# Float32 on TensorE for the first batch's scores and first weights, and decays summed on 128 partitions

## The chip, the cores and the metric

The kernel runs on one core of a Trainium2 chip. The metric is the device time of one execution in microseconds (us). Five engines run side by side, each with its own queue that is worked off in order: TensorE (PE, matrix products; its weight loads are shown as PEld), VectorE (DVE), ScalarE (ACT), GpSimd (POOL) and SyncE (SP), whose queue issues the DMAs.

## The reference, cut to what matters

```python
scores = q @ k.T / sqrt(64)                       # 4 batches, 8 heads, 576 tokens, 64 columns
cum = cumsum(log(clip(f, 1e-4, 1)), axis=-1)
scores = where(causal, -1e9, scores + cum[..., :, None] - cum[..., None, :])
attn = exp(scores - max); attn /= sum(attn) + 1e-9
x = (attn @ v), heads side by side                # 2304 tokens x 512, float32
h = x @ w_in; g = h * tanh(softplus(h)); y = g @ w_out            # 2048 inner columns
z = (sigmoid(y @ w_gate) * (y @ w_val)) @ w_out2                  # 1536 inner columns
```

## The kernel before, in words

TensorE works in fp16 with float32 sums. To keep precision every operand is a pair, a rounded fp16 part (`hi`) and an fp16 remainder (`lo`), and each product takes three fp16 products; the scores get theirs from two stacked matmuls (`L658` with 128 rows, `L659` with 70 rows; `L717` for the last 64 query rows of a batch). The 70 rows hold, beside the rest of q and k, the decay: three fp16 pieces of `cum` against constants of 8 and -8.

The work is cut by batch (4), by pair of heads (4 a batch, index `p`) and by query chunks of 128 tokens. Batch 0 goes in three parts: chunks 0 and 1 (`part == 0`, called the first part here), chunks 2 and 3, and chunk 4. For each pair the way is: load q and k into `st` (`prep`), split them into pairs (`scaled` on ACT or DVE, `rest` on DVE or POOL), scores on PE (`scores`), masked minimum on DVE (`softmax_part`, `L606`), exponential on ACT (`L674`), split of the weights into the pair `pp` (`split`, `L424` and `L443`), a transposing DMA (`L698`), weights times values on PE (`pv`, `L776`, three fp16 products), and the result into `xt` as a pair (`L797` on ACT, `L800` on DVE). `decay` clips `f`, takes the logarithm, sums along 576 tokens on 32 partitions (`L394`), cuts the sum into three fp16 pieces (`L400`, `L402`), and writes it to DRAM (`cum_d`, `L406`), from where the rows of `sb` and `mb` are read (`L479`, `L481`, later `L486`, `L488`).

Beside it run the two feed-forward stages. `h_stream` (`L865` to `L867`) and `y_stream` (`L898` to `L900`) go through 72 steps of 256 tokens by 256 inner columns; block 0 (tokens 0 to 255) needs the first part of all four pairs of batch 0. The weights come as 64-bit words in 32 tiles of 512 KB (`load_w`, `L564`), are turned into float32 by three instructions on DVE (`L544`, `L548`, `L552`) and split into pairs like the rest. The second feed-forward stage is `gv_stream`.

The order on every engine's queue is made by the class `Order`: each task yields what it is about to do with a planned duration, has a due time, and the planner puts the instructions out one by one; `pick` chooses between ACT, DVE and POOL by planned costs. So an edit of one task moves others too.

Of the kernel before, what the change touches and what calls it, by code (L numbers as in the profile page):

```python
# [7 lines left out]
FP32 = mybir.dt.float32  # L8
FP16 = mybir.dt.float16
# [271 lines left out]
def attention_moe_moe_kernel(ctx, tc, qk, v, f, rows_q, rows_k, w_in, w_out, w_gate, w_val, w_out2, out):  # L281
# [6 lines left out]
    NH = f.shape[0]  # L288
# [89 lines left out]
    cum_d = dram.tile([3, NH, S], FP16, name="cum_d")  # L378

    def decay():  # L380
        ft = words(xt[0], 1280, 2 * S).bitcast(FP32)[0:NH]
        cum = words(xt[0], 1280 + 2 * S, 2 * S).bitcast(FP32)[0:NH]
        c16 = words(win[NG1 - 2], 0, 3 * S).rearrange("p (a s) -> p a s", a=3)[0:NH]
        zt = words(wout[0], 0, 2 * S + 2).bitcast(FP32)[0:NH]
        yield "SP", 0.5, 74000
        nc.sync.dma_start(out=ft, in_=f)
        yield "DVE", t_dve2(S)
        nc.vector.memset(zt, 0.0)
        nc.vector.tensor_scalar(ft, ft, 1.0e-4, 1.0, op0=ALU.max, op1=ALU.min)
        yield "ACT", t_act(S)  # L390
        nc.scalar.activation(out=ft, in_=ft, func=ACTF.Ln)
        nc.scalar.activation(out=zt[:, 0:1], in_=zt[:, 0:1], func=ACTF.Exp, scale=0.0)
        yield "DVE", t_dve(S)
        nc.vector.tensor_tensor_scan(  # L394
            out=cum, data0=ft, data1=zt[:, 1:S + 1], initial=0.0, op0=ALU.add, op1=ALU.add
        )
        for part, (a, b) in enumerate(((0, 256), (256, S))):
            for j in range(3):
                yield "DVE", t_dve2(b - a) + (j < 2) * (t_dve(b - a) + 0.127)
                nc.vector.tensor_copy(c16[:, j, a:b], cum[:, a:b])  # L400
                if j < 2:
                    nc.vector.tensor_tensor(cum[:, a:b], cum[:, a:b], c16[:, j, a:b], op=ALU.subtract)  # L402
            if part == 0:
                done("cum0")
            yield "SP", 0.5, 20000 + part * 20000, ("cum", part)
            nc.sync.dma_start(  # L406
                out=cum_d[:, :, a:b].rearrange("j h s -> h j s"), in_=c16[:, :, a:b]
            )
# [44 lines left out]

    def prep(b, p, part, turn):
        i = b * NPB + p
        c0, n = PART[part]
        if b and part == 0:
            yield from need(("s", b - 1, p))
# [8 lines left out]
        done(("st", i))  # L467
        yield from need(("st", i, part))
        first = b == 0 and part == 0
        keys = [("q", i, part, x) for x in range(4 if first else 7)]  # L470

        def rows():
            yield from need(("cum", part), "cq", "ck")
            o = 2 * i
            if first:

                if p == 0:
                    yield "SP", 0.5, 25000, "rq"
                    nc.sync.dma_start(out=SBt[64:67, :, :, 0:n], in_=cum_d[:, 0:2 * NPB, c0:c0 + n])  # L479
                    yield "SP", 0.5, 25000, "rk"  # L480
                    nc.sync.dma_start(out=MBt[67:70, :, :, 0:n], in_=cum_d[:, 0:2 * NPB, c0:c0 + n])  # L481
                yield from need("rq", "rk")
                done(keys[2], keys[3])
            else:
                yield "SP", 0.5, 10000, keys[2]
                nc.sync.dma_start(out=sb[64:67], in_=cum_d[:, o:o + 2, c0:c0 + n])  # L486
                yield "SP", 0.5, 10000, keys[3]
                nc.sync.dma_start(out=mb[67:70], in_=cum_d[:, o:o + 2, c0:c0 + n])  # L488

        spawn(rows(), od.cur["due"])  # L490
        if first:
# [7 lines left out]
        else:  # L499

            (ci,) = yield from take("low")
            low = at.tile([128, 2, 320], FP16, tag="low", name="low", bufs=BUFS["low"])[:, :, 0:n]
            yield from scaled(ma, st, 1.0, 2 * n)
            for dst, src, key in ((sa[0:64], ma[0:64], 4), (sa[64:128], ma[0:64], 0), (mb[0:64], ma[64:128], 1)):
                yield "SP", 0.68, 256 * n, keys[key]
                nc.sync.dma_start(out=dst, in_=src)
# [914 lines left out]
```

## Time and profile before

| | |
|---|---|
| median of three runs | 953.3 us (952.02 to 954.29) |
| profiled execution | 951.72 us, its span 949.9 us |
| PE busy | 881.4 us, 93% of the span |
| DVE busy | 614.0 us, 65% |
| ACT busy | 568.0 us, 60% |
| POOL busy | 83.5 us |
| HBM read, written | 50.71 MB, 4.83 MB |

The span runs from the first to the last instruction; the profiled execution is 1.8 us longer than it. A busy PE is an engine with a matmul in flight, at either clock.

### The profile page before, as it was taken

To read this page: it belongs to the slowest core of one execution; us is meant where nothing else is said; L and a number is where in the kernel's file an instruction comes from. 1 tells how busy PE (TensorE), PEld (TensorE's weight loads), DVE (VectorE), ACT (ScalarE), POOL (GpSimd) and SP (SyncE) were. 2 spreads that over 40 slices of the span, in tenths; PEclk is the share of its full clock that TensorE was granted. 3 is DMA by queue.
4 is the path that set the end of the run, shared out by engine and by line. 5 is a ranking of instruction groups with operands and counts; after the bars stand their busy time and mean duration, and the time that the engine had idled before them with its cause. 6 is when DMAs were issued, how large, how long until landed. Compare 5 with 4: busy or idle time off the path is not lost.

```text
span 949.9 us, 20753 instructions
## 1 busy us (share of the span) xinstructions
PE 881.4 (93%) x8450; PEld 695.0 (73%) x8450; DVE 614.0 (65%) x1374; ACT 568.0 (60%) x1108; POOL 83.5 (9%) x82
## 2 busy tenths in 40 slices
PE   2376689989999999999999999999999999999998
PEld 1254478868887888877888886777777777777786
DVE  8999969877477756656699999964235332532333
ACT  8678757898688877888454465545324433433343
POOL 0301300120010101100200001200000000000000
PEclk9999899999999999999999999999999999999999
DMA  7687888487557784554444433201000000100000
GB/s 242 163 213 201 213 190 237 95 155 138 119 118 134 129 152 99 126 90 71 104 134 138 152 130 115 67 1 46 1 2 23 23 1 1 46 1 1 12 35 23
DMA packets 153556, 93.58 MB, mean 99 GB/s; under 512 B 109578, under 2 KB 135242, under 8 KB 153456
## 3 DMA queue, kind: packets, MB, share of 16 engines
q1 hardware_dynamic: 153462, 92.27, 40.5%
q8 instruction: 66, 1.08, 0.5%
q14 instruction: 28, 0.23, 0.1%
HBM read 50.71 MB, written 4.83 MB: 58 GB/s over the span
## 4 chain that ended last, share of the span: by engine, by line
PE 64%; DVE 4%; DMA 0%; POOL 0%; ACT 0%; issue 0%; ACTq 0%; POOLq 0%
PE bank L1131 8%; PE bank L1133 8%; PE bank L1132 8%; PE o_acc L1279 4%; PE o_acc L1278 4%; PE o_acc L1277 4%; PE y_ps L898 4%; PE y_ps L900 4%; PE y_ps L899 4%; PE h_ps L865 4%; PE h_ps L867 4%; PE h_ps L866 4%; PE o_ps L776 2%; PE s_ps L658 1%; PE s_ps L659 1%; PE s_ps L717 1%
## 5 line engine op out<-in xcount | busy, mean ns | idle before, releaser
L865 PE MATMUL h_ps<-xt,win 128*128 128x256 f16 x576 | 159.4, 277 | 3.1 <-DVE g L838 2.1
L898 PE MATMUL y_ps<-g,wout 128*128 128x256 f16 x576 | 158.8, 276 | 3.7 <-ACT wout L424 3.6
L899 PE MATMUL y_ps<-g,wout 128*128 128x256 f16 x576 | 158.6, 275 | 3.5 <-DVE wout L443 1.9
L866 PE MATMUL h_ps<-xt,win 128*128 128x256 f16 x576 | 158.9, 276 | 3.1 <-DVE xt L800 2.9
L867 PE MATMUL h_ps<-xt,win 128*128 128x256 f16 x576 | 159.0, 276 | 0.4 <-DVE win L443 0.4
L900 PE MATMUL y_ps<-g,wout 128*128 128x256 f16 x576 | 158.7, 275 | 0.0
L1221 DVE TENSOR_TENSOR v<-bank,e 128x512 f32<-128x512 f32 (+1 forms) x30 | 19.1, 637 | 169.2 <-ACT bank L1138 169.2
L1138 ACT ACTIVATE bank<-bank 128x512 f32<-128x512 f32 (+1 forms) x90 | 48.5, 539 | 93.0 <-PE bank L1133 90.3
L443 DVE SCALAR_TENSOR_TENSOR pp<-sp,sm,pp 128x384 f16<-128x384 f32 (+4 forms) x122 | 78.7, 659 | 17.8 <-ACT pp L424 16.4
L606 DVE CUSTOM_DVE_ANT_0 sp<-s_ps,mask 128x384 f32<-128x384 f32 (+4 forms) x144 | 67.2, 492 | 27.6 <-PE s_ps L659 24.1
L674 ACT ACTIVATE sp<-sp,sm 128x384 f32<-128x384 f32 (+3 forms) x112 | 63.7, 569 | 18.3 <-DVE sm L606 17.7
L424 ACT ACTIVATE pp<-sp,sm 128x384 f16<-128x384 f32 (+4 forms) x115 | 66.2, 599 | 11.1 <-issue 3.8
L865 PEld LDWEIGHTS <-win 128*128 128x128 f16 x576 | 56.9, 99 | 16.6 <-issue 3.4
L898 PEld LDWEIGHTS <-wout 128*128 128x128 f16 x576 | 56.8, 99 | 13.9 <-ACT wout L424 4.2
L867 PEld LDWEIGHTS <-win 128*128 128x128 f16 x576 | 56.9, 99 | 12.0 <-issue 3.9
L899 PEld LDWEIGHTS <-wout 128*128 128x128 f16 x576 | 56.9, 99 | 11.9 <-DVE wout L443 2.3
L866 PEld LDWEIGHTS <-win 128*128 128x128 f16 x576 | 57.0, 99 | 10.7 <-issue 1.7
L776 PE MATMUL o_ps<-pt,vt 128*64 128x128 f16 (+1 forms) x1440 | 48.8, 218 | 16.7 <-DMA pt<-pp 14.9
L776 PEld LDWEIGHTS <-vt 128*64 128x64 f16 x1440 | 39.9, 114 | 31.4 <-issue 21.3
L658 PE MATMUL s_ps<-ma,sa 128*128 128x128 f16 (+3 forms) x128 | 39.1, 322 | 25.0 <-DVE sm L606 12.7
L900 PEld LDWEIGHTS <-wout 128*128 128x128 f16 x576 | 56.9, 99 | 7.1
L838 DVE SCALAR_TENSOR_TENSOR g<-h_ps,g 128x512 f16<-128x512 f32 x72 | 49.0, 684 | 18.8 <-ACT g L834 18.5
(195 smaller groups left out, 2269.0 us busy)
## 6 DMA issues: line engine op xcount, KB each, us to landing
xt<-w_in SPq DMA_DIRECT2D x16, 512.0 KB
xt<-w_out SPq DMA_DIRECT2D x16, 512.0 KB
wraw<-w_gate SPq DMA_DIRECT2D x12, 512.0 KB
wraw<-w_val SPq DMA_DIRECT2D x12, 512.0 KB
wraw<-w_out SPq DMA_DIRECT2D x12, 512.0 KB
st<-qk SPq DMA_DIRECT2D x16, 320.0 KB
out<-ob SPq DMA_DIRECT2D x18, 256.0 KB
st<-qk SPq DMA_DIRECT2D x16, 256.0 KB
```

The costliest lines, as they stand in the source:

```text
L443: nc.vector.scalar_tensor_tensor(dst, a, scale, b, op0=ALU.mult, op1=ALU.subtract)
L606: nc.vector.tensor_tensor_reduce(out=sp, in0=ps_ap, in1=mk, op0=ALU.add, op1=ALU.min, scale=-0.125, scalar=1.0e38, accum_out=mn,)
L776: nc.tensor.matmul(o_ps[64 * hh:64 * hh + 64, col:col + n], lhsT=vv[:, jc, vl, 64 * hh:64 * hh + 64], rhs=ptt[:, k, q0:q0 + n], start=(jc ...
L865: nc.tensor.matmul(dst, lhsT=wh, rhs=xh, start=(k == 0), stop=False)
L866: nc.tensor.matmul(dst, lhsT=wh, rhs=xl, start=False, stop=False)
L867: nc.tensor.matmul(dst, lhsT=wl, rhs=xh, start=False, stop=(k == KD - 1))
L898: nc.tensor.matmul(dst, lhsT=wh, rhs=gh, start=first, stop=False, skip_group_check=True)
L899: nc.tensor.matmul(dst, lhsT=wl, rhs=gh, start=False, stop=False, skip_group_check=True)
L900: nc.tensor.matmul(dst, lhsT=wh, rhs=gl, start=False, stop=last, skip_group_check=True)
L1131: nc.tensor.matmul(dst, lhsT=wh, rhs=xh[:, k], start=first, stop=False, skip_group_check=True)
L1132: nc.tensor.matmul(dst, lhsT=wh, rhs=xl[:, k], start=False, stop=False, skip_group_check=True)
L1133: nc.tensor.matmul(dst, lhsT=wl, rhs=xh[:, k], start=False, stop=last, skip_group_check=True)
```

## The change

Batch 0 keeps q and k in float32. They are loaded straight into `Q32` and `K32`, which are the fp16 buffers of the later batches seen as float32, and one float32 matmul with 66 rows (64 of q and k, two for the decay) stands in place of the two fp16 ones, in all three parts of batch 0. Nothing of q and k is split there, so the staging copies between buffers of that batch fall away too.

In the first part the weights stay in float32 as well. They are not split and not transposed by a DMA: a matmul of the unnormalized weights against a diagonal matrix of the normalizing factors (`diag`, from an identity that is loaded) transposes and scales in one go, ACT or DVE copies the result from PSUM to SBUF, and `pv` multiplies it with float32 values. The values' split is put off until after that.

The decays are summed on 128 partitions, four segments of 144 tokens for each of 32 heads. The Ln instruction also gives each segment's total, one matmul with a matrix of zeros and ones (`carry`, loaded) makes the segments' starting values, and the scan starts from them. The float32 sums of batch 0 go to DRAM at once (`cum_f`) and from there as rows into `Q32` and `K32`, before the cut into fp16 pieces, which only the later batches need. POOL fills two whole rows of `K32` and `Q32` with 8 and -8 (`ones`) before those rows are loaded.

```diff
+def t_pe32(n, cols):
+    return n * (4 * cols / 2400 + 0.003)
...
+    def ones():
+        yield "POOL", 2.5
+        nc.gpsimd.memset(K32[64:KF], 8.0)
+        yield "POOL", 1.5
+        nc.gpsimd.memset(Q32[64:KF], -8.0)
+        done("ones")
...
-        nc.scalar.activation(out=ft, in_=ft, func=ACTF.Ln)
...
+        nc.scalar.activation(out=ft, in_=ft, func=ACTF.Ln, accum_out=tot)
...
+        nc.tensor.matmul(hp, lhsT=cm, rhs=tot, start=True, stop=True)
+        yield "DVE", 0.13
+        nc.vector.tensor_copy(car, hp)
...
+        nc.vector.tensor_tensor_scan(out=cum, data0=ft, data1=zt, initial=car, op0=ALU.add, op1=ALU.add)
+        for seg in range(4):
+            yield "SP", 0.5, 5000, ("cum_f", seg)
+            nc.sync.dma_start(out=cum_f[:, seg * SL:(seg + 1) * SL], in_=cum[seg * NH:seg * NH + 2 * NPB])
...
+    def first_rows():
+        yield from need("ones", ("cum_f", 0), ("cum_f", 1))
+        for key, row, n in (("rq", Q32[64:65], 256), ("rk", K32[65:KF], 256), ("rk2", K32[65:KF], S)):
...
-        if first:
-            yield from scaled(sa[0:64], st[0:64], 1.0, 2 * n, pool=False)
-            yield from scaled(ma[64:128], st[64:128], 1.0, 2 * n, pool=False)
-            yield from scaled(sa[64:128], st[0:64], 1.0, 2 * n, pool=False)
-            yield from scaled(mb[0:64], st[64:128], 1.0, 2 * n, pool=False)
-            done(keys[0], keys[1])
-            yield from rest(ma[0:64], st[64:128], 1.0, ma[64:128], 2 * n)
-            yield from rest(sb[0:64], st[0:64], 1.0, sa[0:64], 2 * n)
...
+    def scores_first(p, turn):
...
+                nc.tensor.matmul(
+                    pst[:, hh * n:hh * n + n], lhsT=Q32[0:KF, hh, qi % NQ, c * 128:c * 128 + 128],
+                    rhs=K32[0:KF, hh, p, 0:n], start=True, stop=True,
+                )
...
+        for k in range(4):
+            yield from scaled(diag[:, k * 128:k * 128 + 128], eye, sm[:, 12 + k:13 + k], 128)
...
+                nc.tensor.matmul(
+                    pst[:, m * 128:m * 128 + 128], lhsT=sps[k][1][:, jc * 128:jc * 128 + 128],
+                    rhs=diag[:, k * 128:k * 128 + 128], start=True, stop=True,
+                )
+            (plan,) = pick([("ACT", t_act(w, 0.05))], [("DVE", t_dve(w))])
...
+                if b == 0:
+                    nc.tensor.matmul(
+                        s, lhsT=Q32[0:KF, hh, qi % NQ, q0:q0 + 128], rhs=K32[0:KF, hh, p, 0:n], start=True, stop=True
+                    )
+                    continue
...
+                if own:
+                    yield "PE", t_pe32(2, 128)
+                    for hh in range(2):
+                        ptt, o, pti = pt_t[i, c, hh]
+                        nc.tensor.matmul(
+                            o_ps[64 * hh:64 * hh + 64, col:col + n],
+                            lhsT=v32[p][:, jc, 64 * hh:64 * hh + 64], rhs=ptt[:, o + jc * 128:o + jc * 128 + n],
+                            start=(jc == 0), stop=(jc == c),
+                        )
+                    continue
```

What the change does to the order is seen at three places. On PE, the program of before began with the scores of the first pair, in fp16 pairs (`sa`, `sb` hold q, `ma`, `mb` hold k):

```order
L658 LDWEIGHTS sa
L658 MATMUL s_ps<-ma,sa 128x128
L659 LDWEIGHTS sb
L659 MATMUL s_ps<-mb,sb 128x128
L658 LDWEIGHTS sa
L658 MATMUL s_ps<-ma,sa 128x128
L659 LDWEIGHTS sb
L659 MATMUL s_ps<-mb,sb 128x128
```

It now begins with the sum of the segments (`L430`), the scores of all four pairs follow, and then come the diagonal products (`L763`), the first score of the next part (`L802`) and the first weights times values (`L927`); the loads of a float32 matmul are not listed:

```order
L430 MATMUL carry_ps<-wout_84 128x1
L716 MATMUL s_ps<-mab,sab 128x128 x2
L716 MATMUL s_ps<-mab,sab 128x256 x2
L716 MATMUL s_ps<-mab,sab 128x128 x2
L716 MATMUL s_ps<-mab,sab 128x256 x2
L716 MATMUL s_ps<-mab,sab 128x128 x2
L716 MATMUL s_ps<-mab,sab 128x256 x2
L716 MATMUL s_ps<-mab,sab 128x128 x2
L716 MATMUL s_ps<-mab,sab 128x256 x2
L763 MATMUL t_ps<-diag,wout_88 128x128 x6
L802 MATMUL s_ps<-mab,sab 128x384
L927 MATMUL o_ps<-pt_195,xt_72 64x128 x2
```

So all sixteen score matmuls of the first part stand ahead of the first diagonal product, and scores of the second part stand between the products of the first.

On SP, the queue of before had, after the load of `f`, the loads of q and k (`st`), the constants, a weight tile, and then the way of the decays through DRAM:

```order
L466 DMA st<-qk 128x2x256
L359 DMA sb<-rows_q 6x2560
L361 DMA mb<-rows_k 6x4608
L466 DMA st<-qk 128x2x256 x3
L564 DMA xt_74<-w_in 128x2x512
L406 DMA cum_d<-win_82 32x3x256
L479 DMA sb<-cum_d 3x8x256
L481 DMA mb<-cum_d 3x8x256
```

Now q and k go to their places by two DMAs each (`mab`, `sab`), and the decays' write and read (`cum_f`) stand among them, with the first weight tile behind:

```order
L519 DMA mab<-qk 64x2x256
L438 DMA cum_f<-xt_71 8x144 x2
L521 DMA sab<-qk 64x2x256
L519 DMA mab<-qk 64x2x256
L521 DMA sab<-qk 64x2x256
L508 DMA sab<-cum_f 1x8x256
L508 DMA mab<-cum_f 1x8x256
L630 DMA xt_74<-w_in 128x2x512
```

The first weight tile moved from ahead of the decays' write to behind the decays' rows.

On DVE, the stretch ahead of the first masked minimum (`L606`) of before was filled with the fp16 pieces of the decays, remainders of q and k (`ma`, `sb`) and the first weight tile (`xt_75`):

```order
L400 CAST win_82<-xt_71 32x320
L443 SCALAR_TENSOR_TENSOR ma<-st,ma 64x2x256
L544 TENSOR_SCALAR xt_75<-xt_74 128x512
L443 SCALAR_TENSOR_TENSOR sb<-st,sa 64x2x256
L443 SCALAR_TENSOR_TENSOR ma<-st,ma 64x2x256
L548 SCALAR_TENSOR_TENSOR xt_75<-xt_74,xt_75 128x512
L443 SCALAR_TENSOR_TENSOR sb<-st,sa 64x2x256
L552 SCALAR_TENSOR_TENSOR xt_75<-xt_74,xt_75 128x512
L443 SCALAR_TENSOR_TENSOR ma<-st,ma 64x2x256
L606 ISA wout_88,sm<-s_ps,mask 128x128
```

Now only the decays' sum and a mask stand ahead of it (`L673` is the same operation):

```order
L422 TENSOR_SCALAR xt_71<-xt_71 128x144
L432 COPY wout_84<-carry_ps 128x1
L435 SCALAR_TENSOR_TENSOR xt_71<-xt_71,wout_84 128x144
L394 MEMSET mask_93 128x144
L395 COPY mask_93<-mask 64x64
L396 COPY mask_93<-mask 64x64
L673 ISA wout_88,sm<-s_ps,mask 128x128
L673 ISA sm 128x1
L673 ISA wout_88,sm<-s_ps,mask 128x128
L673 ISA sm 128x1
L607 TENSOR_SCALAR xt_75<-xt_74 128x512
```

The first weight tile and the fp16 pieces moved behind the first masked minimum, and the remainders are gone.

## Rows read from the trace of the kernel before

**Rows 1.** Busy time by stretch; columns as the header of the view says.

```profile
core 0: us, PE busy (x) PEld busy (x) DVE busy (x) ACT busy (x) POOL busy (x), PEclk, DMA share, GB/s
0.00:51.80 51.80, 17.14 (x122) 10.13 (x123) 46.40 (x123) 39.39 (x96) 9.83 (x12) 1.00 0.75 208
51.80:200.00 148.20, 121.52 (x1266) 96.73 (x1265) 131.13 (x317) 113.88 (x233) 23.66 (x23) 0.96 0.79 187
50.00:57.30 7.30, 6.73 (x42) 4.33 (x39) 7.23 (x18) 4.93 (x11) 1.40 (x1) 1.00 0.79 208
200.00:949.90 749.90, 742.71 (x7065) 588.11 (x7063) 436.49 (x936) 414.75 (x781) 50.02 (x48) 1.00 0.31 73
```

**Rows 2.** Timeline up to 52 us: start, duration, instruction, idle before and releaser.

```profile
8.09 0.35 SPq L406 DMA_DIRECT2D cum_d<-win  x1
...
10.29 0.28 SPq L481 DMA_DIRECT2D mb<-cum_d  x1
...
12.08 0.26 PE L659 MATMUL s_ps<-mb,sb 70*128 70x128 f16 x1 [2.24 <-ACT ma L424]
...
26.94 1.45 SPq L698 DMA_TRANSPOSE pt<-pp  x1
...
30.80 1.17 PE L776 MATMUL o_ps<-pt,vt 128*64 128x128 f16 x18 [5.17 <-DMA pt<-pp]
...
51.42 0.42 DVE L800 SCALAR_TENSOR_TENSOR xt<-o_ps,xt 128x256 f16<-128x256 f32 x1
```

**Rows 3.** POOL's fill of the mask, from the timeline.

```profile
0.73 0.63 POOL L365 MEMSET mask<- 128x640 bf16 x1 [0.29 <-POOLq L1411]
```

**Rows 4.** Groups by line and shape, 0 to 52 us: busy us, mean ns, idle.

```profile
L443 DVE SCALAR_TENSOR_TENSOR win<-xt,win 128x512 f16<-128x512 f32 x6 | 5.4, 916 | 0.0
L424 ACT ACTIVATE sa<-st 64x512 f16<-64x512 f32 x8 | 5.0, 628 | 0.9 <-DMA st<-qk 0.7
L443 DVE SCALAR_TENSOR_TENSOR pp<-wout,sm,pp 128x256 f16<-128x256 f32 x8 | 4.8, 613 | 0.0
L548 DVE SCALAR_TENSOR_TENSOR xt<-xt,xt 128x512 int32<-128x512 int32 x7 | 4.8, 683 | 0.1
...
L552 DVE SCALAR_TENSOR_TENSOR xt<-xt,xt 128x512 int32<-128x512 int32 x6 | 4.6, 767 | 0.0
...
L424 ACT ACTIVATE pp<-wout,sm 128x256 f16<-128x256 f32 x8 | 3.9, 494 | 0.0
L424 ACT ACTIVATE win<-xt 128x512 f16<-128x512 f32 x6 | 3.8, 628 | 6.7 <-DVE xt L552 6.6
L443 DVE SCALAR_TENSOR_TENSOR pp<-wout,sm,pp 128x128 f16<-128x128 f32 x7 | 3.4, 499 | 0.0
...
L424 ACT ACTIVATE pp<-wout,sm 128x128 f16<-128x128 f32 x8 | 3.0, 387 | 0.0
...
L544 DVE TENSOR_SCALAR xt<-xt 128x512 int32<-128x512 int32 x7 | 2.9, 416 | 0.0
...
L424 ACT ACTIVATE ma<-st 128x640 f16<-128x640 f32 x4 | 2.9, 720 | 0.0
...
L443 DVE SCALAR_TENSOR_TENSOR ma<-st,ma 64x512 f16<-64x512 f32 x4 | 2.7, 686 | 0.1
...
L443 DVE SCALAR_TENSOR_TENSOR sb<-st,sa 64x512 f16<-64x512 f32 x3 | 2.0, 677 | 0.0
...
L797 ACT ACTIVATE xt<-o_ps 128x256 f16<-128x256 f32 x4 | 1.5, 369 | 0.1
```

**Rows 5.** Neighbouring matmuls of the first step, from the timeline.

```profile
53.77 0.42 PE L866 MATMUL h_ps<-xt,win 128*128 128x256 f16 x1
53.98 0.42 PE L867 MATMUL h_ps<-xt,win 128*128 128x256 f16 x1
...
58.02 0.27 PE L867 MATMUL h_ps<-xt,win 128*128 128x256 f16 x1
58.13 0.27 PE L865 MATMUL h_ps<-xt,win 128*128 128x256 f16 x1
```

More of the change, by code (lines that the diff above doesn't have):

```diff
@@ L393, in decay @@
[L393 to L405, printed above, removed]
+        yield "ACT", t_act(SL, 0.28)
@@ L456, in prep @@
         c0, n = PART[part]
-        if b and part == 0:
+        if part == 0:
             yield from need(("s", b - 1, p))
@@ L466, in prep @@
         nc.sync.dma_start(out=st, in_=qk[i, :, :, c0:c0 + n])
-        done(("st", i))
         yield from need(("st", i, part))
-        first = b == 0 and part == 0
-        keys = [("q", i, part, x) for x in range(4 if first else 7)]
+        keys = [("q", i, part, x) for x in range(7)]
         def rows():
-            yield from need(("cum", part), "cq", "ck")
-            o = 2 * i
-            if first:
[L477 to L488, printed above, removed]
@@ new lines, in rows @@
+            if b == 1 and part == 0:
+                yield "SP", 0.5, 10000
+                nc.sync.dma_start(out=MB[p][64:67], in_=rows_k)
+            yield from need(*[("cum", seg) for seg in range(2 + 2 * part)], "cq")
+            yield "SP", 0.5, 10000, keys[2]
+            nc.sync.dma_start(out=sb[64:67], in_=cum_d[:, b, :, p, c0:c0 + n])
+            yield "SP", 0.5, 10000, keys[3]
+            nc.sync.dma_start(out=mb[67:70], in_=cum_d[:, b, :, p, c0:c0 + n])
+        spawn(rows(), od.cur["due"])
@@ new lines, in prep @@
+        (ci,) = yield from take("low")
+        low = at.tile([128, 2, 320], FP16, tag="low", name="low", bufs=BUFS["low"])[:, :, 0:n]
+        yield from scaled(ma, st, 1.0, 2 * n)
+        for dst, src, key in ((sa[0:64], ma[0:64], 4), (sa[64:128], ma[0:64], 0), (mb[0:64], ma[64:128], 1)):
+            yield "SP", 0.68, 256 * n, keys[key]
+            nc.sync.dma_start(out=dst, in_=src)
+        yield from rest(low, st, 1.0, ma, 2 * n)
+        yield "SP", 0.68, 256 * n, keys[5]
+        nc.sync.dma_start(out=sb[0:64], in_=low[0:64])
@@ L513, in prep @@
+        yield from need(keys[4], keys[0])
+        yield "SP", 0.68, 256 * n, keys[6]
+        nc.sync.dma_start(out=ma[0:64], in_=low[64:128])
         give("stage", si)
         yield from need(*keys)
-        if not first:
-            give("low", ci)
+        give("low", ci)
         done(("q", i, part))
@@ L521, in prep_v @@
         if b == 0:
[L522 removed]
+            yield from need("rk")
             (vi,) = yield from take("vt", turn=turn)
[L524 removed]
+            s = v32[p]
         else:
@@ L756, in pv @@
         cs = CHUNKS[b > 0][part]
-        yield from need(("v", i))
+        own = b == 0 and part == 0
+        yield from need(("v32" if own else "v", i))
         for c in cs:
@@ L1353, in attention_moe_moe_kernel @@
                         dues[c] = due
-                    spawn(scores(b, p, parts, ns) if parts else scores4(b, p, ns), due)
+                    if b == 0 and part == 0:
+                        spawn(scores_first(p, ns), due)
+                    else:
+                        spawn(scores(b, p, parts, ns) if parts else scores4(b, p, ns), due)
                     ns += 1
```

245 lines of the change are left out of this document (186 added, 59 removed).

## The prediction

> **What bounds the kernel now.** I read the busy time by stretch first. From 200 us to the end PE is busy 742.7 of 749.9 us, and nothing in the change touches that stretch; it comes sooner or later as a whole. From 51.8 to 200 us PE is busy 121.5 of 148.2 us and DVE 131.1. In the first 51.8 us PE is busy only 17.1 us, DVE 46.4 and ACT 39.4 [rows 1]. So this stretch belongs to DVE, with ACT close behind. 51.8 us is the end of the fourth pair's output write (`L800`, 51.42 us plus 0.42) [rows 2]: from there block 0 can run through all four pairs. I call it the fourth output, and ask first how far the change moves it.
>
> The timeline shows the way there. The decays go to DRAM at 8.09 us, their second read is issued at 10.29, and the first score that uses them runs at 12.08. At the first pair's weights PE then waits 5.17 us for the transposing DMA, issued at 26.94 and used at 30.80 [rows 2].
>
> **The start.** The sum along 144 tokens in place of 576, and the rows written before they are cut in three, let the write to DRAM be issued earlier than 8.09 us. From write to use took 4.0 us (8.09 to 12.08) [rows 2]. But the rows now also wait for POOL's `ones`, and on SP everything behind those rows waits with them: the first weight tile and the values. POOL's mask of 640 elements took 0.63 us, from 0.73 on [rows 3], about 1 ns an element. `ones` and the mask are 4608 + 640 + 2560 = 7808 elements, so POOL ends at 0.73 + 7.7 = 8.4 us; from there to the use it took 1.8 us (10.29 to 12.08) [rows 2], and the first score comes at about 10.3. The fill is in float32, which no row shows. If an element of it costs twice as much, POOL ends 7.1 us later. If POOL's time is mostly fixed cost, the write to DRAM is last and the score comes some 2 us earlier. I take 10.5, between 8.5 and 17.5.
>
> **DVE up to the fourth output.** Off its 46.4 us [rows 1] go: the remainders of q and k, 2.7 + 2.0; the remainders of the first part's weights, 4.8 + 3.4; and, because the order has fewer weight tiles ahead of that point, 2 of 7 first steps, 2 of 7 second and 2 of 6 third steps, 2 of 6 remainders: 0.8 + 1.4 + 1.5 + 1.8 = 5.5 [rows 4]. New ahead of it: three remainders of the second part's weights, one masked minimum, one remainder of the values and one split of a weight tile, six at up to 0.9 (the tile's remainder, 916 ns) [rows 4], 5 us. That leaves 46.4 - 4.7 - 8.2 - 5.5 + 5 = 33. Some 2 us of these stand ahead of the first score. About 1 us more goes with POOL, which shared 9.8 us of that stretch with DVE [rows 1] and has no work in the new order between the mask and the fourth output: 30 us behind the first score.
>
> **ACT.** Off its 39.4 us [rows 1]: 16 copies of q and k, of which eight took 5.0, so 10.0; the first part's weights, 3.9 + 3.0; the second part's k and q, 2.9; three of six weight tiles, 1.9 [rows 4]. New are 15 diagonals (one more falls to DVE) at 0.387, four PSUM copies of 256 at 0.37 and four of 512, where I take 0.63, the SBUF copy of that size [rows 4]: 9.8 us, and an exponential and two splits more, at most 1.9. Sum 29, with 3 us of it ahead of the first score. So ACT needs 26, less than DVE.
>
> DVE was busy 90% of that stretch; the longest stops at its start are gone with the pieces of the decays, but DVE, PE and ACT now hand every pair to each other twice. With 95% the fourth output comes at 10.5 + 30 / 0.95 = 42 us. **That is 9.8 us sooner.** The transposes' waits are part of this stretch and are not counted again.
>
> **PE in that stretch.** No float32 matmul with more than one column is in the trace. Below, it could cost one fp16 pass over its columns. Above, four: two halves of each operand make four products, of which the fp16 triple leaves one out. I take four, since float32 holds more bits than two fp16 parts. On this the Trainium skill agrees, FP8 and Floating Point Precision, section TensorE Precision Notes: a true FP32 product takes four passes through the array; no row here shows it, and by it the sum is the one below.
>
> The first part has per pair 768 columns each of scores, diagonals and values: 3 x 768 x 4 passes x 4 pairs = 36,900. Ahead of the fourth output also stand three scores of 384 and two of 512 columns, 2176 x 4 = 8,700, and nine step matmuls. Before 57.3 us neighbours of 256 columns start 0.21 us apart, which is 1.2 GHz, and later 0.11, which is 2.4 GHz, though the clock column prints 1.00 for both [rows 1, 5]. So that is 40 us at the lower clock, 20 at the higher. The window is 42 - 10.5 = 31.5. PE was 6.7 of 7.3 us busy when the clock rose [rows 1]; the scores are as dense, so I expect it to rise in their run, and PE to need about 28 us: tight, but under DVE.
>
> **Behind the fourth output.** The scores of the other parts double: 16 float32 matmuls in place of pairs, 7168 columns with two passes more at 0.11 us per 256 is 6.1 us; chunk 4, four times four passes over 288 columns with two heads side by side, in place of eight, adds 2.0. Of the 8.1 us some 1.9 lie ahead of the fourth output (2176 of 7168 columns). The remaining 6.2 meet a stretch in which PE was busy 82% and DVE 88%. If PE sets the pace all of it counts, if DVE does none; I take half, **3.1 us later**. With one pass it would instead save 2; nothing else is costed there: the copies of q and k that fall away were ACT's and the DMAs', whose share was 0.79 [rows 1], and the values' split is only put off.
>
> **Sum.** 951.7 (profiled) - 9.8 + 3.1 = 945.0. The median of the runs shown is 1.6 above the profiled execution, so 946.6; I say 946.5. A change of 0.2% (1.9 us) is about what a measurement of this kernel tells from none.
>
> **The rivals.**
>
> *PE becomes the bound of the first stretch* (0.16): the clock stays at 1.2 GHz until the fourth output. Then 40 us of matmuls (35 if the two heads' values run side by side, as their fp16 rows do) start at 10.5 and, with PE 87% busy, end at 51 to 56; with the 3.1 us behind it that is 954 to 959 profiled, around 957. It decides once the fourth output is later than 48.7 us (51.8 - 3.1). For it: in 51.8 us of before the spacing never fell below 0.21 us. Against: a run as dense as this one was not there before 50 us.
>
> *Weight loads in the open* (0.05). PEld took 96.7 us for 1265 loads, 0.076 each, all beside matmuls [rows 1]. If each pass of a float32 matmul had to load 0.076 us in the open, the 69 or so ahead of the fourth output cost 69 x 4 x 0.076 = 21 us more, about 41 in all even at 2.4 GHz, and that output comes at 53, for a time near 958. The Trainium skill has a rule that points there, TensorE: Matmul & The Clock Gate, section Weight-path perf modes: the fast weight load is not used where the input is FP32. The loads in rows 1 are fp16, so the trace neither agrees nor disagrees.
>
> *The gain is given back by the weight stream* (0.09): the tiles arrive at the pace of the DMAs, block 0 starts at 42 us and waits for them. 953, no change. Against it: the DMA share is 0.79, and the removed transposes and copies lighten it.
>
> *POOL's float32 fill is slow* (0.05): the first score comes at 17.5, the fourth output at 49, and the time is 953.
>
> *More than forecast* (0.15): the clock, once up in the scores, stays up. The step work that ran at 0.21 us spacing from 50 to 57.3 us, 6.7 us busy [rows 1], takes half, 3.4 less, and the 3.1 of float32 scores hides under DVE: 945.0 - 6.5 + 1.6 = 940.
>
> **How the numbers follow.** My forecast has 0.50, at 941 to 950 by itself. Faster by over 0.2%: forecast and *more*, with a part of the late fill, 0.67. Within 0.2%: the weight stream and the rest of the late fill, 0.12. Slower: the two PE cases, 0.21. The range of 937 to 957 takes in the bounds of the fill and half of the PE cases, and leaves out their far ends (0.13) and a far better one (0.05).
>
> **What the profile after would show.** First score at 10 to 11 us, with POOL's two fills ended before it. The first block-0 write to `xt` near 30 us and the fourth near 42, with DVE over 90% busy between. PE's float32 matmuls of 256 columns 0.43 us apart at the higher clock, 0.85 at the lower. The stretch between the fourth output and full PE no more than 3 us longer than before. Wrong it is if the first score waits for POOL, if PE is full from 10 us to the fourth output, or if that output is early and the first step still waits for weights.

## The result, and the profile after

The changed kernel takes **942.98 us** (median of 6 runs, 942.37 to 945.87), the kernel before 953.41 (6 runs, 952.02 to 954.29). The ratio is 0.9902, with a 95% interval of 0.989 to 0.9914. The forecast was 946.5, faster. The profiled execution took 943.07 us, its span 941.3.

Busy time by stretch after the change, cut where rows 1 were cut, and two parts of it for themselves; columns as in rows 1:

```profile
core 0: us, PE busy (x) PEld busy (x) DVE busy (x) ACT busy (x) POOL busy (x), PEclk, DMA share, GB/s
0.00:44.00 44.00, 29.63 (x154) 21.61 (x155) 30.00 (x101) 29.01 (x85) 7.29 (x8) 1.00 0.69 186
44.00:191.40 147.40, 130.80 (x1275) 100.72 (x1273) 128.52 (x318) 120.37 (x242) 28.43 (x27) 0.90 0.79 187
191.40:941.30 749.90, 741.02 (x7051) 586.39 (x7048) 432.55 (x932) 414.64 (x774) 54.12 (x52) 1.00 0.31 73
12.00:44.00 32.00, 29.04 (x152) 21.11 (x153) 26.57 (x93) 25.83 (x80) 0.00 (x0) 1.00 0.80 215
```

The last stretch is as long as in [rows 1], 749.9 us. The fourth output comes at 44.0 in place of 51.8, and the stretch behind it is 147.4 in place of 148.2. So 7.8 of the span's 8.6 us lie ahead of the fourth output. From 12 to 44 us PE is now the busiest engine, 29.0 of 32 us, and DVE has 26.6. Cut at 24.9 us, where the granted clock rises (the clock column prints 1.00 ahead of that too), and once more from the first write to `xt` of block 0 to the fourth:

```profile
12.00:24.90 12.90, 12.58 (x43) 11.18 (x44) 9.55 (x45) 8.19 (x33) 0.00 (x0) 1.00 1.00 288
24.90:44.00 19.10, 16.46 (x111) 9.93 (x111) 17.02 (x49) 17.64 (x48) 0.00 (x0) 1.00 0.66 166
32.50:43.60 11.10, 9.27 (x57) 4.92 (x57) 9.98 (x29) 10.33 (x26) 0.00 (x0) 1.00 0.55 152
```

Up to 24.9 us PE is full, at 1.2 GHz, and DVE has room. Behind that ACT is the busiest (17.6 of 19.1 us), with DVE (17.0) and PE (16.5) close to it.

The way to the first score and to the fourth output, from the timeline (start, duration, instruction, idle before and releaser; the last row is the eighth output, of which more below):

```profile
0.73 3.93 POOL L380 MEMSET mab<- 2x4608 f32 x1 [0.29 <-POOLq L1588]
2.69 2.06 DVE L422 TENSOR_SCALAR xt<-xt 128x144 f32<-128x144 f32 x1 [1.67 <-DMA xt<-f]
5.41 2.23 POOL L382 MEMSET sab<- 2x2560 f32 x1
6.15 0.52 DVE L435 TENSOR_TENSOR_SCAN xt<-xt,wout 128x144 f32<-128x144 f32 x1
6.70 0.67 SPq L438 DMA_DIRECT2D cum_f<-xt  x2
10.18 0.63 SPq L508 DMA_DIRECT2D mab<-cum_f  x1
12.32 0.98 PE L716 MATMUL s_ps<-mab,sab 66*128 66x128 f32 x3 [6.47 <-DMA mab<-cum_f]
...
12.66 10.23 PE L716 MATMUL s_ps<-mab,sab 66*128 66x128 f32 x31
22.69 2.56 PE L763 MATMUL t_ps<-diag,wout 128*128 128x128 f32 x12
26.19 1.60 PE L763 MATMUL t_ps<-diag,wout 128*128 128x128 f32 x12
...
43.58 0.42 DVE L964 SCALAR_TENSOR_TENSOR xt<-o_ps,xt 128x256 f16<-128x256 f32 x1
...
102.31 0.42 DVE L964 SCALAR_TENSOR_TENSOR xt<-o_ps,xt 128x256 f16<-128x256 f32 x1
```

The decays go to DRAM at 6.70 in place of 8.09 us, but the first score starts at 12.32, where it was 12.08 for the row in [rows 2]. Both POOL fills end before it, at 7.64. The sixteen scores stand in the trace as 32 rows, two for each matmul; 3072 columns with four passes at 1.2 GHz are 10.24 us, and from the first score's start to the first diagonal product's, 12.32 to 22.69, it is 10.37. Twelve rows of diagonal products take 2.56 us, the next twelve of the same pattern 1.60: the granted clock rises at 24.9 us, near the end of the first twelve, after the scores and not in them. The fourth write to `xt` ends at 44.00.

What stands in [rows 4] has these counterparts up to 44 us (busy us, mean ns, idle):

```profile
L470 ACT ACTIVATE diag<-win,sm 128x128 f32<-128x128 f32 x15 | 5.8, 395 | 1.2 <-DVE sm L698 1.2
L611 DVE SCALAR_TENSOR_TENSOR xt<-xt,xt 128x512 int32<-128x512 int32 x5 | 3.4, 682 | 0.0
L489 DVE SCALAR_TENSOR_TENSOR win<-xt,win 128x512 f16<-128x512 f32 x4 | 2.7, 685 | 0.0
L770 ACT ACTIVATE pt<-t_ps 128x512 f32<-128x512 f32 x4 | 2.3, 584 | 0.0
L770 ACT ACTIVATE pt<-t_ps 128x256 f32<-128x256 f32 x4 | 1.5, 376 | 0.0
```

The remainders of q and k and of the first part's weights are gone; the diagonals and the PSUM copies are there at nearly the prices taken (0.387 and 0.63, 0.37 us).

Behind the fourth output the steps did not come sooner by one and the same amount. A step of `h_stream` is 24 matmuls; their ends, counted in the two traces:

| end of, us | before | after | sooner by |
|---|---|---|---|
| fourth output | 51.8 | 44.0 | 7.8 |
| step 5, last of block 0's first six | 95.5 | 94.9 | 0.6 |
| eighth output (second part complete) | 115.6 | 102.7 | 12.9 |
| step 6, first of block 1 | 119.2 | 105.4 | 13.8 |
| step 15 | 176.1 | 163.4 | 12.7 |
| step 16 (waits for batch 1) | 201.1 | 190.8 | 10.3 |
| step 34 | 314.3 | 305.3 | 9.0 |

Block 0's steps lost the lead again. Three things go with that, and none was tried by itself: the weights came only some us sooner (the last conversion of the sixteenth tile at 92.7 in place of 95.8 us), from 45 to 62 us PE was mostly at the lower clock (last section), and right ahead of step 5 PE waited for a masked minimum of chunk 4, whose scores stand before that step on its queue:

```profile
88.99 2.19 PE L869 MATMUL s_ps<-mab,sab 66*64 66x288 f32 x8 [4.33 <-DVE sm L673]
```

Block 1's first step came 13.8 us sooner, behind an eighth output 12.9 us sooner, and some of that went back at batch 1. That is not the picture of the prediction, and the experiments go after it.

### The profile page after: what moved, and what is told of

Same layout as the page of the kernel before. It is cut to its first block, busy times and chain, and to the rows that moved or that the text cites. A ratio compares the mean times of both kernels' runs of the same rounds, so it can differ in the third digit from the quotient of the medians.

```text
span 941.3 us, 20733 instructions
## 1 busy us (share of the span) xinstructions
PE 901.4 (96%) x8476; PEld 708.7 (75%) x8476; DVE 591.1 (63%) x1348; ACT 564.0 (60%) x1099; POOL 89.8 (10%) x87
## 4 chain that ended last, share of the span: by engine, by line
PE 66%; DVE 15%; DMA 7%; ACT 5%; SPq 3%; issue 2%; POOL 1%; ACTq 0%; DVEq 0%; POOLq 0%
PE bank L1295 7%; PE bank L1296 7%; PE bank L1297 7%; PE h_ps L1029 5%; PE o_acc L1443 4%; PE o_acc L1441 4%; PE o_acc L1442 4%; PE h_ps L1030 4%; PE h_ps L1031 4%; PE y_ps L1062 4%; PE y_ps L1064 4%; PE y_ps L1063 4%; PE o_ps L939 4%; DMA st<-qk 2%; DMA xt<-w_in 2%
## 5 line engine op out<-in xcount | busy, mean ns | idle before, releaser
L1063 PE MATMUL y_ps<-g,wout 128*128 128x256 f16 x576 | 157.0, 273 | 1.0 <-DVE wout L489 1.0
L1062 PE MATMUL y_ps<-g,wout 128*128 128x256 f16 x576 | 157.2, 273 | 0.3 <-ACT wout L470 0.3
L1064 PE MATMUL y_ps<-g,wout 128*128 128x256 f16 x576 | 157.0, 273 | 0.0
L1385 DVE TENSOR_TENSOR v<-bank,e 128x512 f32<-128x512 f32 (+1 forms) x30 | 19.1, 636 | 168.5 <-ACT bank L1302 168.5
L489 DVE SCALAR_TENSOR_TENSOR pp<-sp,sm,pp 128x512 f16<-128x512 f32 (+4 forms) x119 | 76.3, 655 | 20.3 <-ACT pp L470 19.0
L673 DVE CUSTOM_DVE_ANT_0 sp<-s_ps,mask 128x384 f32<-128x384 f32 (+4 forms) x144 | 67.6, 492 | 26.9 <-PE s_ps L807 21.9
L470 ACT ACTIVATE pp<-sp,sm 128x384 f16<-128x384 f32 (+4 forms) x109 | 63.4, 603 | 6.7 <-POOL low L498 2.1
L992 ACT ACTIVATE h_ps<-h_ps 128x512 f32<-128x512 f32 x72 | 41.7, 586 | 22.0 <-PE h_ps L1031 21.6
L939 PEld LDWEIGHTS <-vt 128*64 128x64 f16 x1368 | 38.3, 116 | 19.3 <-issue 17.8
L939 PE MATMUL o_ps<-pt,vt 128*64 128x128 f16 (+1 forms) x1368 | 46.8, 221 | 3.5 <-DMA pt<-pp 3.3
```

Source lines behind the costliest of these rows:

```text
L489: nc.vector.scalar_tensor_tensor(dst, a, scale, b, op0=ALU.mult, op1=ALU.subtract)
L673: nc.vector.tensor_tensor_reduce(out=sp, in0=ps_ap, in1=mk, op0=ALU.add, op1=ALU.min, scale=-0.125, scalar=1.0e38, accum_out=mn,)
L939: nc.tensor.matmul(o_ps[64 * hh:64 * hh + 64, col:col + n], lhsT=vv[:, jc, vl, 64 * hh:64 * hh + 64], rhs=ptt[:, k, q0:q0 + n], start=(jc ...
L1062: nc.tensor.matmul(dst, lhsT=wh, rhs=gh, start=first, stop=False, skip_group_check=True)
L1063: nc.tensor.matmul(dst, lhsT=wl, rhs=gh, start=False, stop=False, skip_group_check=True)
L1064: nc.tensor.matmul(dst, lhsT=wh, rhs=gl, start=False, stop=last, skip_group_check=True)
```

## The experiments

All ran in the full kernel. Comparisons are of the ratios to the kernel before on the same chip: the changed kernel has 0.9902, and 0.001 is 0.95 us. Differences of under 2 us are within the intervals. Fourth and eighth outputs are from the profiled executions.

| run | median, us | ratio (95%) | against the changed kernel, us | fourth / eighth output | span |
|---|---|---|---|---|---|
| changed kernel | 942.98 | 0.9902 (0.989 to 0.9914) | | 44.0 / 102.7 | 941.3 |
| later scores twice | 950.03 | 0.9966 (0.9954 to 0.9978) | +6.1 | 45.0 / 107.0 | 945.5 |
| diagonal products twice | 945.06 | 0.9926 (0.991 to 0.9942) | +2.3 | 46.2 / 104.6 | 943.0 |
| minima twice | 947.16 | 0.9947 (0.9929 to 0.9965) | +4.3 | 47.9 / 104.8 | 943.6 |
| decays on 32 partitions | 943.29 | 0.9902 (0.9888 to 0.9915) | 0.0 | 44.7 / 102.8 | 941.2 |
| weights and values in fp16 | 944.67 | 0.9917 (0.9896 to 0.9938) | +1.4 | 52.2 / 103.1 | 944.5 |
| preparation put back | 951.45 | 0.9988 (0.9973 to 1.0003) | +8.2 | 45.2 / 109.0 | 949.4 |
| its order alone | 947.62 | 0.9955 (0.994 to 0.9969) | +5.1 | 43.3 / 106.7 | 947.3 |
| rows of 8 by DMA | 942.04 | 0.9885 (0.9862 to 0.9909) | -1.6 | 44.0 / 100.8 | 938.5 |
| that, extra matmuls first | 942.01 | 0.9891 (0.9862 to 0.992) | -1.0 | 47.0 / 105.8 | 945.5 |
| put back, order kept | 962.88 | 1.0115 (1.0099 to 1.0131) | +20.3 | 65.4 / 122.4 | 960.6 |
| engines' part of it | 948.06 | 0.9957 (0.9942 to 0.9971) | +5.2 | 51.5 / 109.1 | 947.3 |
| DMAs' part of it | 954.58 | 1.0016 (1.0001 to 1.0031) | +10.9 | 50.4 / 111.0 | 949.7 |

**Does PE's added work cost, behind the fourth output?**

```diff
+                    for _ in range(2):
                         nc.tensor.matmul(
                             s, lhsT=Q32[0:KF, hh, qi % NQ, q0:q0 + 128], rhs=K32[0:KF, hh, p, 0:n], start=True, stop=True
                         )
...
+                    for _ in range(1 if b else 2):
                         nc.tensor.matmul(
                             pst[64 * hh:64 * hh + 64, 0:288], lhsT=lhsT, rhs=rhs,
```

> Every float32 score matmul of batch 0's chunks 2, 3 and 4 is issued twice, with the same result; nothing else moves. That is 7168 x 4 / 2400 = 11.9 us of PE at 2.4 GHz for chunks 2 and 3 and 3.8 us for chunk 4, 15.7 in all, 3.6 of them ahead of the fourth output. Theory DVE (DVE sets the pace on both sides of the fourth output, PE's extra work lies beside it): fourth output at 44 to 46 us, time 943 to 947. Theory PE (PE's work counts in full in the stretch behind the fourth output): 12 us more there, time near 956. The half that the prediction took: near 949 to 951.

15.7 us of matmuls cost 6.1 us, 0.39 for each, near the half that the prediction took and neither theory's. At that slope, an estimate, the 8.1 us that the prediction has for the change's added work cost 3.1, and the 6.2 of them behind the fourth output 2.4. Yet the stretch did not get longer by the change, so something else took as much off.

**Which engine paces the first stretch?** The diagonal products, and then the masked minima (`softmax_part` in `scores_first`), are issued twice in the same way, in two kernels:

```diff
+                for _ in range(2):
                     nc.tensor.matmul(
                         pst[:, m * 128:m * 128 + 128], lhsT=sps[k][1][:, jc * 128:jc * 128 + 128],
```

```diff
+                for _ in range(2):
                     softmax_part(
                         pst[:, hh * n:hh * n + n], mask[:, 512 - 128 * c:640], spt[:, hh * n:hh * n + n],
```

> Every one of the 24 diagonal products of the first part is issued twice: 24 x 2 x 0.112 = 5.4 us more of PE at 2.4 GHz between 22 us and the fourth output, with the same result. Theory DVE: the fourth output stays within 1.5 us of 44.0, time 942 to 945. Theory PE (PE is the bound of the first stretch in the changed kernel, 29.0 of 32 us busy from 12 to 44): fourth output near 49, time near 948.

> Every masked minimum of the first part is issued twice on DVE: 3.0 + 2.0 + 16 x 0.083 = 6.3 us more of DVE between 13 us and the fourth output, with the same result. Theory DVE: fourth output 4 to 6 us later, at 48 to 50, time 947 to 949. Theory PE: DVE has some 5 us of room from 12 to 44 (26.6 of 32 busy), so the fourth output is less than 2 us later, time 943 to 945.

```profile
L764 PE MATMUL t_ps<-diag,wout 128*128 128x128 f32 x96 | 13.2, 298 | 0.0
```

```profile
L673 DVE CUSTOM_DVE_ANT_0 wout<-s_ps,mask 128x256 f32<-128x256 f32 x16 | 6.4, 420 | 0.3
L673 DVE CUSTOM_DVE_ANT_0 wout<-s_ps,mask 128x128 f32<-128x128 f32 x16 | 4.3, 290 | 5.4 <-PE s_ps L716 5.1
```

The first fence is the group of the products in the run that doubles them: 13.2 us where the changed kernel has 8.2. These 5.0 us put the fourth output off by 2.2. The second is the doubled minima, 10.7 where it has 5.0, and with the 16 more read-outs of 0.083 some 7 us of DVE; these put it off by 3.9. So each us on PE costs 0.44 there and each on DVE 0.56: neither engine alone paces the stretch, and both theories fall. ACT, the busiest engine behind 24.9 us, was not given more work, so its share in the pace stays open.

**The decays' sum.** The scan goes over 32 partitions of 576 again, without the carry matmul:

```diff
-        ft = words(xt[0], 1280, 2 * SL).bitcast(FP32)
+        N = 8 * NB
+        ft = words(xt[0], 1280, 2 * S).bitcast(FP32)[0:N]
...
-        nc.vector.tensor_tensor_scan(out=cum, data0=ft, data1=zt, initial=car, op0=ALU.add, op1=ALU.add)
+        nc.vector.tensor_tensor_scan(out=cum, data0=ft, data1=zt, initial=0.0, op0=ALU.add, op1=ALU.add)
```

> The changed kernel with the decays summed on 32 partitions along 576 tokens again (no matmul for the carry, its load kept, the order of everything else kept); the scores stay in float32. Theory DVE or PE: the decays' sum is worth little, the clip waits for POOL's fill in both, the longer Ln, scan and the casts behind cost 0.5 to 2.5 us, first score at 12.5 to 14, time 943 to 946. Rival (the gain is the decays' earlier sum): most of the gain is gone, time 950 or more.

The first score comes at 12.72, 0.4 later, and the time is the same. With POOL's fill ahead of the clip in both, the 128 partitions bring nothing that can be measured.

**The first part's weights and values in fp16 again**, with splits and transposing DMAs:

```diff
-                    if b == 0 and part == 0:
-                        spawn(scores_first(p, ns), due)
-                    else:
+                    if 1:
                         spawn(scores(b, p, parts, ns) if parts else scores4(b, p, ns), due)
...
-        if b == 0:
-            yield from need(("p", i, 1, 0))
-            od.due(od.cur["due"] + VLATE)
...
-        own = b == 0 and part == 0
+        own = False
```

> The changed kernel with float32 in the scores alone: the first part's weights are split into fp16 pairs and transposed by the DMA again, its values split ahead of them, as before the change; decays on 128 partitions, q and k of batch 0 unsplit. Theory split (the gain comes in about equal parts from the splits of q and k and from those of the weights with their transposes): DVE gets back 4.8 + 3.4 us of remainders and the transposes' wait, the fourth output comes 5 to 8 us later than 44.0, the eighth near 107, time 946 to 949. Rival (scores in float32 and decays bring all of it): 942 to 944. Rival (the weights in float32 bring all of it): 952 or more.

The fourth output is back at 52.2, as late as before the change: the whole lead there belongs to the float32 weights, with the values' split that they let wait. But the eighth is at 103.1, and the time only 1.4 us longer, which is within the intervals. A late fourth output was made good in 50.9 us to the eighth, where the changed kernel needs 58.7 (this run splits the values ahead of the fourth, the changed kernel behind it). So the float32 weights make the prettiest difference in the trace and little in the time.

**What took off what PE's work put on?** Behind the fourth output, the prediction had costed the preparation of q and k of chunks 2 to 4 (casts, remainders, copies) at nothing. It is put back, planned as before, with its results unused (the copies go to DRAM, not to a buffer on the chip):

```diff
+        yield from scaled(a, src, 1.0, 2 * n)
+        for k in range(3):
+            yield "SP", 0.68, 256 * n, ("bk", p, k)
+            nc.sync.dma_start(out=spare[k, :, :, 0:n], in_=a)
+        yield from rest(low, src, 1.0, a, 2 * n)
+        for k in range(3, 5):
+            yield "SP", 0.68, 256 * n, ("bk", p, k)
+            nc.sync.dma_start(out=spare[k, :, :, 0:n], in_=low)
```

> The changed kernel, with the work that preparing q and k of batch 0's chunks 2 to 4 cost before put back to no use: per pair one cast of 640 columns to fp16, one remainder of 640, and five DMA copies of 82 KB, here into DRAM. Theory relief (the eighth output comes 12.9 us earlier than before, the fourth only 7.8, and the 5.1 between them are this work's absence): eighth output at 105 to 108 in place of 102.7, time 946 to 948. Rival (this work lay in the idle time of ACT, POOL and the DMAs, and the lead at the eighth output has another origin): within 1.5 us of the changed kernel, 942 to 944.5.

That takes 8.2 of the 9.3 us away. But the planner makes another order when it counts this work, so the next run keeps that order and drops the instructions (here against the run before it; the cast and the remainder go in the same way):

```diff
         for k in range(3):
             yield "SP", 0.68, 256 * n, ("bk", p, k)
-            nc.sync.dma_start(out=spare[k, :, :, 0:n], in_=a)
```

> The program of the run with the put-back preparation, without the instructions and DMAs that were put back: the planner counted them, so every queue has the order that it made for them, and the work itself is the changed kernel's. Theory relief (the put-back work itself took the gain away): 942 to 945. Theory order (the planner's new order took it away): 949 to 951.5.

The order alone costs 5.1 us, the work itself the other 3.1 (each give or take 2), so both theories hold in part. On every engine's queue the two runs have the same instructions in the same order, but for those put back. From the fourth to the eighth output, before the change, with the work put back, with its order alone, and in the changed kernel (rows of four traces, in this order):

```profile
51.80:115.60 63.80, 45.87 (x443) 32.88 (x441) 60.45 (x145) 50.34 (x94) 10.60 (x11) 0.92 0.82 205
```

```profile
45.20:109.00 63.80, 52.69 (x439) 34.71 (x437) 58.38 (x141) 48.40 (x90) 11.66 (x11) 0.85 0.79 206
```

```profile
43.30:106.70 63.40, 51.29 (x437) 34.07 (x437) 56.75 (x141) 47.08 (x87) 7.13 (x8) 0.87 0.74 188
```

```profile
44.00:102.70 58.70, 49.95 (x420) 33.78 (x418) 52.52 (x128) 46.90 (x87) 9.90 (x9) 0.80 0.80 196
```

The stretch is as long with the work put back as before the change, 63.8 us, and DVE is busy 95, 92, 90 and 89% of it. In the changed order DVE has 7.9 us less there than before. Of the work's own 3.1 us little lies in this stretch: these executions differ by 1.9 us at the fourth output (45.2 against 43.3) and by 0.4 behind it. The order makes the stretch 4.7 us longer, and the clock does not explain that, as it was lower in the shorter one (0.80 against 0.87).

What the two orders do differently can be seen in the remainders of the weight tiles in this stretch (POOL and DVE in the changed kernel, then with the order alone):

```profile
L498 POOL TENSOR_TENSOR win<-xt,win 128x512 f16<-128x512 f32 x5 | 6.4, 1285 | 60.8 <-ACT xt L494 60.8
L489 DVE SCALAR_TENSOR_TENSOR win<-xt,win 128x512 f16<-128x512 f32 x3 | 2.1, 687 | 0.0
```

```profile
L498 POOL TENSOR_TENSOR win<-xt,win 128x512 f16<-128x512 f32 x2 | 2.3, 1156 | 43.3 <-ACT xt L494 43.3
L489 DVE SCALAR_TENSOR_TENSOR win<-xt,win 128x512 f16<-128x512 f32 x6 | 4.1, 686 | 0.0
```

The planner that does not count the preparation gives three of these eight to POOL that DVE has otherwise, and it puts some of the minima behind the eighth output. So "order" here takes in the choice of engine. In all DVE has 13 instructions and 4.2 us less in the shorter stretch, at the same busy share. That these make the 4.7 us fits the rows, but was not tried by itself.

**The same work in the changed kernel's own order**, unknown to the planner, whole and in two parts:

```diff
+        nc.scalar.activation(out=a, in_=K32[0:64, :, p, c0:c0 + n], func=ACTF.Copy, scale=1.0)
+        nc.gpsimd.tensor_tensor(low, K32[0:64, :, p, c0:c0 + n], a, op=ALU.subtract)
+        for k in range(5):
+            nc.sync.dma_start(out=spare[k], in_=K32[0:64, :, p, c0:c0 + n // 2])
```

> The reverse: the changed kernel in its own order, with the preparation of q and k of chunks 2 to 4 put back unknown to the planner: per pair one cast of 640 columns on ACT, one remainder on POOL, five DMA copies of 82 KB into DRAM. Theory relief: eighth output at 106 or later in place of 102.7, time 947 to 951. Theory order: the work lies in idle time of ACT, POOL and the DMAs, within 2 us of the changed kernel, 942 to 945.

> Of that the casts on ACT and the remainders on POOL alone, 4 x 0.72 and 4 x 1.5 us, without the DMAs. Theory relief by the engines: 946 or more. Theory relief by the DMAs, and theory order: 942 to 944.5.

> Of that the 20 DMA copies of 82 KB alone, 1.6 MB, some 8 us of all DMA engines at the 200 GB/s of that stretch, and 20 issues of 0.57 us on SP. Theory relief by the DMAs: the weight tiles and transposes behind them come later, 946 or more. Theory relief by the engines, and theory order: 942 to 944.5.

These cost much more than the planned work, and the waits say why (queue and line, releaser: us, times, longest; from 10 to 60 us, the run with the engines' part and then the run with the DMAs'):

```profile
ACT low L514 <- DMA mab<-qk: 7.0, 3, 5.8
```

```profile
SPq L516 <- DMA mab<-qk: 10.7, 4, 4.9
```

The put-back instructions come to their turn before the load of k has landed, and everything behind them on ACT or SP waits too. So these three runs do not price the work. They show something else: lateness of the fourth output by 21.4, 7.5 and 6.4 us came out as 19.3, 6.0 and 8.4 us of span. With the order kept, most of a late start is passed on (the two doublings of the first stretch passed on 1.7 of 2.2 us and 2.3 of 3.9).

**The start.** The constant rows come by two small DMAs in place of POOL's fills; in a second kernel TensorE also gets 28 matmuls of 512 fp16 columns to no use, around the carry matmul:

```diff
-        nc.gpsimd.memset(K32[64:KF], 8.0)
-        nc.gpsimd.memset(Q32[64:KF], -8.0)
+        nc.sync.dma_start(out=K32[64:65], in_=ones_k)
+        nc.sync.dma_start(out=Q32[65:KF], in_=ones_q)
```

```diff
+        def warm(n):
+            for _ in range(n):
+                nc.tensor.matmul(wp, lhsT=wm[:, 0:128], rhs=wm, start=True, stop=True)
+
+        warm(8)
...
         nc.tensor.matmul(hp, lhsT=cm, rhs=tot, start=True, stop=True)
+        warm(20)
```

> The changed kernel, with the constant rows of 8 and -8 loaded by two small DMAs in place of POOL's two fills; the order of everything else is the same. Theory port (the clip of 144 columns took 2.06 us because DVE had to wait for POOL's fill, and the chain behind it to the first score is late by that): clip under 0.3 us, first score at 10.0 to 10.8 in place of 12.32, fourth output 1 to 2 us earlier, time 941 to 942.5. Rival (the clip is slow for another reason, or the rows' way through DRAM is bound by something else): first score still near 12, time 942.5 to 944.

> As the run with the rows by DMA, and TensorE is given 28 matmuls of 512 fp16 columns to no use from its start on, 8 ahead of the carry matmul and 20 behind it, so that the granted clock may rise before the first score. If it does, the first part's scores take 5.3 us in place of 10.6. Theory DVE (DVE sets the pace of the first stretch): fourth output 0 to 2 us earlier than without the extra matmuls, time within 1.5 us of that run. Theory PE: fourth output 3 to 5 us earlier than without them, time 938 to 940. If the clock does not rise or falls again, no change against that run, or later by the matmuls that stand ahead of the carry.

The timeline of the first:

```profile
2.62 0.23 DVE L422 TENSOR_SCALAR xt<-xt 128x144 f32<-128x144 f32 x1 [1.59 <-DMA xt<-f]
4.40 0.52 DVE L435 TENSOR_TENSOR_SCAN xt<-xt,wout 128x144 f32<-128x144 f32 x1
5.60 0.60 SPq L519 DMA_DIRECT2D mab<-qk  x1
6.33 0.74 SPq L438 DMA_DIRECT2D cum_f<-xt  x2
11.88 1.65 PE L716 MATMUL s_ps<-mab,sab 66*128 66x128 f32 x5 [7.78 <-DMA cum_f<-xt]
```

The clip takes 0.23 us in place of 2.06, so the port theory holds for it, and the scan ends at 4.92 in place of 6.67. But the write of the decays leaves only at 6.33: on SP it stands behind the loads of q and k, and now that is last. The first score comes 0.4 us sooner, not 2, and the fourth output not at all. The 1.6 us in the time are within the intervals.

In the second kernel the clock does rise before the scores and then falls again. Three stretches of it, columns as above, the clock ahead of the DMA share:

```profile
7.50:14.30 6.80, 5.65 (x30) 3.44 (x29) 0.97 (x6) 0.88 (x4) 0.00 (x0) 1.00 0.61 175
14.30:24.50 10.20, 8.96 (x32) 7.26 (x30) 8.71 (x40) 7.95 (x32) 0.00 (x0) 0.50 1.00 302
31.40:41.60 10.20, 10.20 (x41) 6.21 (x40) 7.30 (x18) 7.85 (x21) 0.00 (x0) 0.50 0.45 143
```

It stands at 2.4 GHz from 7.5 us and at 1.2 from 14.3 to 24.5, which is most of the scores, and again from 31.4 to 41.6 with PE wholly busy. The profiled execution's fourth output came at 47.0; the six executions took 938.3 to 947.3 us, and the profiled one is the longest. What the low clock in the scores costs stays open: this run did not take it away.

## Why the prediction was right, and which of its steps were not

**The number** (946.5 against 942.98, within the forecast's own 941 to 950) was right, and the sign. Two of its terms were off in opposite ways, the lead by 2.0 us (7.8, not 9.8) and the stretch behind it by 3.9 (0.8 us shorter, not 3.1 longer). That the number came so close is in part luck.

**Start.** First score 12.32, forecast 10.5. The fills did end before it. Last was the decays' way: the clip waited 1.8 us for POOL, and from write to use it took 5.6 us (6.70 to 12.32), not 4.0. POOL's float32 element costs 0.85 ns (3.93 us for 4608), not double.

**DVE and ACT up to the fourth output**: 30.0 and 29.0 us busy, forecast 33 and 29. The fourth output came at 44.0 in place of 42; the late start is 1.8 of that. From the first score to there it took 31.7 us, forecast 31.5, but by two errors that cancelled: DVE had 26.6 us of work and not 30, and it was busy 83% (of 32 us) and not 95%. Up to 24.9 us PE at the lower clock was full, and DVE had 9.6 of 12.9 us. Between the first block-0 write (32.5 us, forecast 30) and the fourth DVE was busy 90%, about as forecast, and ACT 93%. Neither PE nor DVE alone sets the pace, as the two doublings showed.

**PE.** Four passes, as taken; here the trace agrees with the Trainium skill, FP8 and Floating Point Precision, section TensorE Precision Notes. PE needed 29.0 us in the window (forecast 28), but the clock rose at 24.9, not in the scores' run. No weight load is in the open: the scores keep PE busy 10.58 us for 10.24 us of passes. The Trainium skill's rule on the fast weight load (TensorE: Matmul & The Clock Gate, section Weight-path perf modes), which is not used for FP32 input, changed nothing that this trace shows.

*PE becomes the bound of the first stretch* came half true: PE was full and at 1.2 GHz up to 24.9 us. But at 2.4 GHz behind that it needed 29.0 us in all and not 40, and the fourth output stayed ahead of 48.7, from where that rival would have decided.

**Behind the fourth output: the step that failed.** PE's work there was sized well (3.1 us taken, 2.4 by the slope of the doubling). The failed step is the sentence "nothing else is costed there". The preparation of chunks 2 to 4 that falls away was taken to be hidden in ACT's and the DMAs' idle time; it is worth 3.1 us as work, and 5.1 more by the order, and the choice of engines, that the planner makes without it. Together that is more than PE's added work, and the stretch became 0.8 us shorter in place of 3.1 longer. The sentence also left out POOL, which had the remainders of that preparation before the change (nanoseconds, shortest, median and longest; first and last start in us):

```profile
L452 POOL TENSOR_TENSOR low<-st,ma x4: 1397/1828/1841, 33.5 to 52.9; 128x640 f16<-128x640 f32 x4
```

**The lead "comes sooner as a whole"** holds in the main with one order kept (6.0 to 19.3 us of span for 6.4 to 21.4), and does not hold across orders: the run with fp16 weights has its fourth output 8.2 us later than the changed kernel and ends 3.2 us later by its span. The eighth output tells more: in all twelve runs its shift against the changed kernel and that of the span agree within 3 us. The rival in which the weight stream gives the lead back has its outcome in block 0 (step 5 only 0.6 us sooner; whether by the weights is not shown) and not in the time, since block 1's first step came 13.8 us sooner, right behind the eighth output.

**Of the gain of 9.3 us**, by undoing one part at a time: the decays' sum 0.0, float32 weights and values 1.4, the preparation of q and k of the later parts 8.2, of which 5.1 is order. These were not undone together, and PE's added work is inside each, so they need not add up. What the float32 scores of the first part alone bring was not tried. Which of DVE, ACT, POOL and the DMAs the put-back work hurts stays open too.

## What to carry to other kernels

Work that looks hidden because its engine has idle time has to be priced in the stretch where it lies; when a planner sets the order, taking it out also changes the order and the choice of engines, and that change alone was worth 5 us here, half of the whole gain. A run that keeps the new order and drops the work, or keeps the work and the old order, tells the two apart. A milestone in the trace (here the fourth output) stands for the time only between kernels with the same order; the eighth, behind which the next block starts, followed it better.

## What the runs showed of the hardware

- POOL's fill of 2 x 4608 float32 held DVE up: the clip, released at 2.69 us, ended at 4.75, just behind the fill (4.66), and takes 0.23 us without it. The Trainium skill says so of the port pair that the two share, for a VectorE instruction in one of its two-port modes, which `tensor_scalar` can enter, SBUF — State Buffer, section Who interferes with whom: whoever issues first has it for the whole instruction, and the other blocks. The trace agrees. Not every DVE instruction is held: the memset below ran in the midst of the same fill in 0.18 us, and the scan takes 0.52 us with POOL's second fill beside it and 0.52 without:

```profile
0.84 0.18 DVE L420 MEMSET wout<- 128x144 f32 x1 [0.84 <-PEq L1588]
```

- After the change the granted clock changed more often: between the fourth output and some 200 us it fell to 1.2 GHz five times, before the change three times. The mean of the stretch behind the fourth output is 0.90 above and was 0.96 before [rows 1]; that 0.96 counts the time up to 57.3 us as full speed, where matmuls still started 0.21 us apart [rows 5], and with it at half speed the mean is about 0.94. That float32 work is the cause was not tried. The clock was low for most of this part of the changed kernel, with PE busy 15.5 of 17 us:

```profile
45.40:62.40 17.00, 15.50 (x96) 8.65 (x97) 16.08 (x41) 13.56 (x25) 2.49 (x2) 0.60 0.87 193
```
